# A front end's steps issued one per half step from its beginning (batches 3 to 7) in a fused attention, Fourier and feed-forward kernel

## The chip, the cores and the metric

The kernel runs on one core of a Trainium2 chip. The metric is the device time of one execution in microseconds (us), as the median of several runs. The engines are PE (TensorE), DVE (VectorE), ACT (ScalarE), POOL (GpSimd) and SP (SyncE, which here issues nearly all DMAs). Each engine works through its own list of instructions in the order of the list.

## The reference

For each of 8 batches (576 tokens, 8 heads of width 64): keys and values are averaged over groups of 8 tokens, softmax attention is done against the 72 pooled keys, and the heads' outputs are put side by side to x (576 x 512). Then:

```python
X = np.fft.fft(np.fft.fft(x, axis=1), axis=2)
u = x + np.real(X)
un = (u - mean(u)) / sqrt(var(u) + 1e-6)
out = u + relu(un @ w_ch1) @ w_ch2          # 512 -> 2048 -> 512
```

## The kernel before, in words

**Two kinds of work.** The *feed-forward* work (function `ffn`) is a chain of blocks over token columns. A block has 16 slices of the hidden dimension; each slice has a first product (`g`, line 687, 12 matmuls) and a second one (`acc`, line 671, 12 matmuls). One such dozen is a **half step**. Every product is split into high and low parts (unh, unl for the activations, w1h/w1low and w2h/w2low for the weights), so 12 matmuls are 3 combinations by 4 chunks. The low weight parts are read back from DRAM for each slice (`w1low`, `w2low`, line 210).

The *front end* of a batch (generator `fe(b)`) does the attention, the Fourier part and the normalisation. Its steps end at each `yield`. PE's parts of it have names by stage, with the batch's number: psS (scores), psT, psV, psR (transposes), psX (values), psA and psB (channel transform), psQ and psP (sequence transform), psM (mean), psVar (variance). 20 steps lead to `yield "U"`; before it nothing of the batch's half of the ring is written. Behind it come psQ, then psP (at its last one `yield "free"`), then the mean step with `centre`, and the variance with three Newton steps.

**The ring.** U, unh and unl hold two batches side by side (1152 columns). After batch 0, blocks of 384 columns run over the ring: three blocks for batches 1 and 2 (half steps 64 to 159), three for 3 and 4 (160 to 255), three for 5 and 6 (256 to 351), and two blocks of 288 for batch 7 (352 to 415). The middle block of a round needs the columns of both batches: half steps 192 and 288 are the first that need batch 4 and batch 6. Batch 4's half of the ring is free from half step 160 on, batch 6's from 256 on (table `free`, line 709).

**What a front end does behind psP.** When the last psP matmul is done: X takes the transform (L565, L566 on DVE), POOL makes the sums and differences in U (L582, L583), DVE adds the two even parts (`s`, L575), ACT and DVE split that sum (L577, L578), PE forms the mean in two column halves (psM, L598 and L599), DVE subtracts it half by half (X, L600), ACT rounds the four tiles to unh (L590), and unl is the rest (L591: tiles 0 and 1 on DVE, tiles 2 and 3 on POOL). The first products of the block then use unh and unl.

**The order.** The driver loop (line 769 on) runs through the half steps; after each, `advance(pos)` lets every running front end go on until its count of steps reaches `upto`. A front end begins when the one before it yields "free". Behind "U" it goes one step per half step from `free[b]` on, in both versions. The framework's scheduler then orders each engine's list: it places a front end's instruction where it reckons it ready, so the lists do not stand exactly as the program was written.

Of the kernel before, what the change touches and what calls it, by code (L numbers as in the profile page):

```python
# [80 lines left out]
def tile_kernel(ctx: ExitStack, tc: tile.TileContext, qt, kt, vm, vr, w1, w2, cad, cbd, mkd, out):  # L81
# [627 lines left out]
    free = {1: 0, 2: 64, 3: 128, 4: 160, 5: 224, 6: 256, 7: 320}  # L709
    npre = 20  # L710
# [31 lines left out]
    def start(b, pos):  # L742
        if b < B:
            run[b] = [fe(b), 0, pos, None]

    def advance(pos):
        for b in sorted(run):
            r = run[b]
            if r[3] is None:
                upto = (pos + 1 - r[2]) * npre / max(free[b] - 1 - r[2], 24)  # L750
            else:
                upto = r[3] + pos - max(free[b], r[2]) + 1 if pos >= free[b] else 0
            while r[1] < upto:
                said = next(r[0], "end")
                r[1] += 1
                if said == "U":
                    r[3] = r[1]
                    r[2] = pos
                    break
                if said == "free":  # L760
                    start(b + 1, pos)
                if said == "end":
                    del run[b]
                    break
# [4 lines left out]
    pos = 0  # L769
    for blk in blocks():  # L770
        for _ in ffn(*blk):
            for _ in range(2):
                if done_w < need(pos):
                    prep_w(done_w)
                    done_w += 1
            advance(pos)
            pos += 1
# [109 lines left out]
```

## Time and profile before

| | |
|---|---|
| median of 3 runs | 1124.24 us (1123.67 to 1126.21) |
| the profiled execution's own time | 1127.34 us |
| its span, first to last instruction | 1125.6 us |
| granted TensorE clock, mean | 0.965 |
| PE busy | 1051.0 us (93%), 6484 matmuls |
| DVE, ACT, POOL busy | 629.9, 421.2, 253.1 us |

Times of instructions are counted from the span's start. A row of a timeline gives start, duration, engine, line, operation, output<-inputs and how many followed each other; in square brackets stands how long the engine was idle before, and what ended it. Matmuls are pipelined: the time that one takes from the next is the distance of their starts, not the duration in the row. A row of windows gives the busy time of each engine in a stretch, the granted clock, the DMA share and GB/s.

### The profile page before, as it was taken

How to read it: one execution, taken by the hardware profiler on the slowest of the kernel's cores; microseconds unless marked ns; L12 is line 12 of the kernel's file. 1: busy time of each engine (PE TensorE's matmuls, PEld its weight loads, DVE VectorE, ACT ScalarE, POOL GpSimd, SP SyncE). 2: the span in 40 equal slices, each digit the busy share in tenths (PEclk: the TensorE clock that was granted, in tenths of full speed). 3: DMA queues.
4: the chain of work that ended last, by engine and by line, in shares of the span. 5: the costliest groups of instructions: out<-in, count | busy, mean ns of one | idle time of the engine just before them, and what ended most of it. 6: DMA issues, size and time to landing. Idle time of an engine off the chain costs nothing.

```text
span 1125.6 us, 17476 instructions
## 1 busy us (share of the span) xinstructions
PE 1051.0 (93%) x6484; PEld 1010.6 (90%) x6484; DVE 629.9 (56%) x1228; ACT 421.2 (37%) x1140; POOL 253.1 (22%) x256
## 2 busy tenths in 40 slices
PE   6657898999999999999979999999997999999997
PEld 5446877999999999999968999999986999999997
DVE  7686886856366463664548456565467544353122
ACT  6577864443233332333314333144333342131110
POOL 4473355301140022300232003220024000120000
PEclk8568999999999999999989999999998999999999
DMA  6748987655434454445533446345452434345563
GB/s 221 255 155 258 302 296 232 193 182 163 128 117 149 145 157 132 122 143 153 150 102 106 122 126 195 102 117 160 135 173 58 117 101 133 91 124 180 167 189 97
DMA packets 91877, 175.79 MB, mean 156 GB/s; under 512 B 10128, under 2 KB 17296, under 8 KB 91536
## 3 DMA queue, kind: packets, MB, share of 16 engines
q1 hardware_dynamic: 91504, 172.01, 49.4%
q0 software_dynamic: 288, 2.66, 0.6%
q8 instruction: 51, 0.84, 0.3%
q14 instruction: 34, 0.28, 0.1%
HBM read 156.81 MB, written 17.83 MB: 155 GB/s over the span
## 4 chain that ended last, share of the span: by engine, by line
PE 78%; DVE 6%; DMA 5%; POOL 4%; ACT 3%; issue 3%; SPq 0%; DVEq 0%; POOLq 0%; ACTq 0%
PE acc L671 32%; PE g L687 32%; PE psS L327 3%; PE psX L408 3%; DMA k<-in_kt 2%; PE psA L517 2%; DMA wst<-in_w 1%; PE psP L550 1%; PE psB L533 1%; PE psT L365 1%; POOL U L582 1%; DVE wd L195 1%; POOL k L262 1%; POOL U L583 1%; PE psQ L550 1%
## 5 line engine op out<-in xcount | busy, mean ns | idle before, releaser
L692 DVE SCALAR_TENSOR_TENSOR hl<-g,hh 128x384 fp32r<-128x384 f32 (+1 forms) x208 | 108.5, 522 | 205.2 <-ACT hh L691 201.1
L691 ACT ACTIVATE hh<-g 128x384 fp32r<-128x384 f32 (+1 forms) x208 | 96.6, 465 | 299.5 <-PE g L687 286.7
L671 PE MATMUL acc<-hh,w2h 128*128 128x384 f32 (+1 forms) x832 | 191.4, 330 | 3.5 <-DVE U L702 2.8
L671 PE MATMUL acc<-hh,w2low 128*128 128x384 f32 (+1 forms) x832 | 188.5, 327 | 0.0
L671 PE MATMUL acc<-hl,w2h 128*128 128x384 f32 (+1 forms) x832 | 180.9, 327 | 2.0 <-DVE hl L692 1.9
L687 PE MATMUL g<-unh,w1low 128*128 128x384 f32 (+1 forms) x832 | 176.7, 329 | 4.7 <-DMA w1low<-w1l 4.7
L687 PE MATMUL g<-unl,w1h 128*128 128x384 f32 (+1 forms) x832 | 176.4, 328 | 2.7 <-DVE unl L591 2.1
L687 PE MATMUL g<-unh,w1h 128*128 128x384 f32 (+1 forms) x832 | 174.6, 328 | 0.0
L671 PEld LDWEIGHTS acc<-hh,w2h 128*128 128x128 f32 x832 | 142.7, 189 | 6.9 <-ACT hh L691 3.0
L687 PEld LDWEIGHTS g<-unh,w1low 128*128 128x128 f32 x832 | 140.7, 190 | 6.6 <-DMA w1low<-w1l 5.5
L687 PEld LDWEIGHTS g<-unl,w1h 128*128 128x128 f32 x832 | 140.5, 189 | 6.0 <-DVE unl L591 3.4
L671 PEld LDWEIGHTS acc<-hh,w2low 128*128 128x128 f32 x832 | 143.8, 189 | 0.2
L671 PEld LDWEIGHTS acc<-hl,w2h 128*128 128x128 f32 x832 | 140.3, 189 | 3.3 <-DVE hl L692 3.1
L687 PEld LDWEIGHTS g<-unh,w1h 128*128 128x128 f32 x832 | 140.4, 190 | 0.4
L344 POOL TENSOR_TENSOR t<-t,sm 128x720 f32<-128x720 f32 x32 | 44.8, 1401 | 258.3 <-DVE sm L343 227.7
L262 POOL TENSOR_TENSOR k<-k 128x288 f32<-128x288 f32 (+1 forms) x56 | 38.7, 690 | 94.4 <-DMA k<-in_kt 69.3
L327 PE MATMUL psS<-kpb,q 128*128 128x144 f32 x280 | 45.9, 305 | 6.6 <-DVE X L600 6.4
L582 POOL TENSOR_TENSOR U<-X,U 128x576 f32<-128x576 f32 (+1 forms) x16 | 23.5, 1480 | 118.9 <-DVE X L566 118.9
L327 PEld LDWEIGHTS psS<-kpb,q 128*128 128x128 f32 x280 | 42.6, 206 | 8.0 <-DVE X L600 7.0
L329 DVE TENSOR_REDUCE mx<-psS 128x6 f32<-128x432 f32 x64 | 33.3, 527 | 15.7 <-PE psS L327 15.3
L341 DVE TENSOR_REDUCE sm<-t 128x10 f32<-128x720 f32 x28 | 25.2, 899 | 16.9 <-ACT t L340 16.5
L517 PE MATMUL psA<-ca,f 128*128 128x258 f32 (+1 forms) x144 | 25.3, 307 | 8.9 <-ACT f L477 8.9
(205 smaller groups left out, 1442.5 us busy)
## 6 DMA issues: line engine op xcount, KB each, us to landing
w1low<-w1l SPq DMA_DIRECT2D x208, 256.0 KB, 2.7
w2low<-w2l SPq DMA_DIRECT2D x208, 256.0 KB, 2.9
wst<-in_w SPq DMA_DIRECT2D x30, 512.0 KB, 5.1
q<-in_qt SPq DMA_DIRECT2D x28, 288.0 KB, 3.1
k<-in_kt SPq DMA_DIRECT2D x28, 288.0 KB, 2.9
v<-in_vm SPq DMA_DIRECT2D x28, 256.0 KB, 2.9
out<-U SPq DMA_DIRECT2D x18, 384.0 KB, 3.7
w1l<-wd SPq DMA_DIRECT2D x16, 256.0 KB, 4.7
```

What stands on the lines that cost most here:

```text
L262: nc.gpsimd.tensor_tensor(out=out if n == 1 else src[:, :, 0:n], in0=src[:, :, 0] if n == 1 else src[:, :, 0:n], in1=src[:, :, 1] if n == ...
L327: nc.tensor.matmul(ps[:, c * W2J:(c + 1) * W2J], lhsT=q[:, r0:r0 + P], rhs=kpb[g % 2], start=True, stop=True)
L329: nc.vector.tensor_reduce(out=mx[:, c0:c0 + n], in_=pv, op=ALU.max, axis=AX.X, negate=b in SM)
L341: nc.vector.tensor_reduce(out=sm, in_=t, op=ALU.add, axis=AX.X)
L344: ins = nc.gpsimd.tensor_tensor(out=t, in0=t, in1=sm.unsqueeze(3).broadcast_to([P, 5, 2, J]), op=ALU.mult)
L408: nc.tensor.matmul(ps, lhsT=w, rhs=a, start=(i == 0), stop=(i == len(mm) - 1))
L517: nc.tensor.matmul(ps, lhsT=w, rhs=a, start=(n == 0), stop=(n == len(mm) - 1))
L582: engine(1 - j, UE).tensor_tensor(out=a, in0=e, in1=o, op=ALU.add)
L671: nc.tensor.matmul(acc[e], lhsT=w[:, e], rhs=h, start=(f == f0 and x == 0), stop=(f == f1 - 1 and x == 2))
L687: nc.tensor.matmul(ps, lhsT=w[:, c], rhs=x[:, ti, cl], start=(n == 0), stop=(n == 11))
L691: nc.scalar.activation(hh, ps, AF.Relu)
L692: nc.vector.scalar_tensor_tensor(out=hl, in0=ps, scalar=0.0, in1=raw(hh), op0=ALU.max, op1=ALU.subtract)
```

## The change

Only the number of steps that `advance` allows before "U" is changed:

```diff
             if r[3] is None:
-                upto = (pos + 1 - r[2]) * npre / max(free[b] - 1 - r[2], 24)
+
+                upto = (pos + 1 - r[2]) * (npre / (free[b] - 1) if b == 2 else 1)
             else:
                 upto = r[3] + pos - max(free[b], r[2]) + 1 if pos >= free[b] else 0
```

`r[2]` is the half step at which the front end began, `npre` is 20. Batch 2 began before the loop (`r[2]` is 0), and its number stays what it was. By the program, batch 3 begins at half step 67 and reached "U" at 127, and now at 86; batch 4 begins at 131 and reached it at 159, now at 150; batch 5 begins at 163: 223, now 182; batch 6 begins at 227: 255, now 246; batch 7 begins at 259: 319, now 278. No instruction is added or removed.

In PE's list, counted in half steps (feed-forward matmuls that stand ahead, divided by 12), the stages stand here:

| batch | first psS | first psT | last psB | psP_2 | last psM |
|---|---|---|---|---|---|
| 3 before, now | 92.4, 87.0 | 102.1, 99.8 | 135.9, 131.3 | 141.1, 136.5 | 144.8, 140.2 |
| 4 before, now | 141.1, 136.5 | 156.3, 148.7 | 189.9, 181.8 | 192.0, 186.9 | 192.0, 190.6 |
| 5 before, now | 192.0, 186.9 | 201.1, 199.2 | 235.9, 230.2 | 241.1, 235.3 | 244.8, 239.0 |
| 6 before, now | 241.1, 235.3 | 256.3, 247.7 | 288.0, 279.4 | 288.0, 284.6 | 288.0, 288.0 |
| 7 before, now | 288.0, 284.6 | 297.2, 295.0 | 330.7, 325.2 | 335.8, 330.4 | 339.2, 333.6 |

PE's list at the block that first needs batch 4 (g1_2112_0 and g1_2112_1 are its first two first products, acc1728 is the block ahead, psS5 batch 5's scores), before:

```order
L550 MATMUL psP4_2_5718<-cb_71,A0_5462 128x290 x3
L550 MATMUL psP4_2_5718<-cb_71,A1_5463 128x290 x3
L550 MATMUL psP4_2_5718<-cb_71,AB2_5464 128x290
L598 MATMUL psM4_5779<-s_5750,avg_74 128x288
L598 MATMUL psM4_5783<-s_5750,avg_74 128x288
L599 MATMUL psM4_5779<-s_5751,avg_74 128x288
L599 MATMUL psM4_5783<-s_5751,avg_74 128x288
L327 MATMUL psS5_3_0_5832<-kpb1_76,q5_3_5761 128x144 x3
L327 MATMUL psS5_3_3_5838<-kpb1_76,q5_3_5761 128x144 x2
L687 MATMUL g1_2112_0_6501<-unh_83,w1h_68 128x384
L687 MATMUL g1_2112_1_6548<-unh_83,w1h_68 128x384
```

and now, from the same stage on:

```order
L550 MATMUL psP4_2_5718<-cb_71,A0_5351 128x290 x3
L550 MATMUL psP4_2_5718<-cb_71,A1_5352 128x290 x3
L550 MATMUL psP4_2_5718<-cb_71,AB2_5353 128x290
L327 MATMUL psS5_3_0_5776<-kpb1_76,q5_3_5761 128x144 x3
L671 MATMUL acc1728_0_3_5623<-hl_6547,w2h6_2090 128x384
L687 MATMUL g1_1728_14_6599<-unh_83,w1h7_2013 128x384 x4
L687 MATMUL g1_1728_14_6599<-unl_84,w1h7_2013 128x384 x4
L687 MATMUL g1_1728_14_6599<-unh_83,w1low_6562 128x384 x4
L671 MATMUL acc1728_0_0_5620<-hh_6579,w2h6_2090 128x384
L671 MATMUL acc1728_0_1_5621<-hh_6579,w2h6_2090 128x384
```

Before, no feed-forward matmul stood between psP4_2 and the block's first products; now 61 do, with the four psM4 and psS5's ten among them. At the block of batch 6 (g1_3264) it stood before as at batch 4's, with all of psQ6 and the last two tiles of psB6 also behind the old block's last matmul; now psP6_2 stands like this:

```order
L671 MATMUL acc2880_0_2_8290<-hh_9247,w2low_9199 128x384
L550 MATMUL psP6_2_8386<-cb_71,A0_8019 128x290 x3
L550 MATMUL psP6_2_8386<-cb_71,A1_8020 128x290 x3
L550 MATMUL psP6_2_8386<-cb_71,AB2_8021 128x290
L327 MATMUL psS7_3_0_8444<-kpb1_76,q7_3_8429 128x144 x3
L671 MATMUL acc2880_0_3_8291<-hh_9247,w2low_9199 128x384
L671 MATMUL acc2880_0_0_8288<-hl_9248,w2h6_2090 128x384
L671 MATMUL acc2880_0_1_8289<-hl_9248,w2h6_2090 128x384
```

and 41 feed-forward matmuls, four psM6 and ten psS7 stand between it and g1_3264's first.

DVE's list at the same place. Before, from the end of batch 6's mean on (L600 subtracts it, L591 is unl, L329 and L338 belong to batch 7's scores):

```order
L578 TENSOR_TENSOR s_8419<-s_8417,s_8418 128x576
L600 TENSOR_TENSOR X_80<-U_81,psM6_8447 128x4x288
L600 TENSOR_TENSOR X_80<-U_81,psM6_8451 128x4x288
L329 TENSOR_REDUCE mx_8498<-psS7_3_0_8500 128x6
L591 TENSOR_TENSOR unl_84<-X_80,unh_83 128x576
L338 TENSOR_TENSOR t7_3_8497<-psS7_3_0_8500,mx_8498 128x432
L591 TENSOR_TENSOR unl_84<-X_80,unh_83 128x576
```

Now the first L600 is followed by a sum of batch 7 (L341) and the four L701 of the block that ends, and from the last of these on it reads:

```order
L701 TENSOR_TENSOR acc2880_0_3_8291<-acc2880_0_3_8291,rb_82 128x384
L600 TENSOR_TENSOR X_80<-U_81,psM6_8478 128x4x288
L342 TENSOR_SCALAR sm_8443<-sm_8443 128x10
L702 TENSOR_TENSOR U_81<-U_81,acc2880_0_0_8288 128x384
L329 TENSOR_REDUCE mx_8550<-psS7_2_0_8552 128x6
L702 TENSOR_TENSOR U_81<-U_81,acc2880_0_1_8289 128x384
L702 TENSOR_TENSOR U_81<-U_81,acc2880_0_2_8290 128x384
L702 TENSOR_TENSOR U_81<-U_81,acc2880_0_3_8291 128x384
L343 RECIPROCAL sm_8443<-sm_8443 128x10
L591 TENSOR_TENSOR unl_84<-X_80,unh_83 128x576
L338 TENSOR_TENSOR t7_2_8549<-psS7_2_0_8552,mx_8550 128x432
L591 TENSOR_TENSOR unl_84<-X_80,unh_83 128x576
```

So the eight instructions that end the old block (L701, L702) stood ahead of batch 6's psQ work before, and now stand among its last instructions.

## The prediction

> **What bounds the kernel now.** I read the page's first two parts, then a table of windows, then PE's waits.
>
> ```profile
> span 1125.6 us, 17476 instructions
> PE 1051.0 (93%) x6484; PEld 1010.6 (90%) x6484; DVE 629.9 (56%) x1228; ACT 421.2 (37%) x1140; POOL 253.1 (22%) x256
> PEclk8568999999999999999989999999998999999999
> ```
>
> The clock falls twice after the start, in slices 21 and 31. Windows around these places:
>
> ```profile
> 250.00:566.00 316.00, 316.00 (x1914) 311.08 (x1914) 173.27 (x346) 108.73 (x296) 61.93 (x62) 1.00 0.47 142
> 606.00:833.00 227.00, 227.00 (x1375) 223.69 (x1374) 124.46 (x247) 79.20 (x220) 38.03 (x40) 1.00 0.46 140
> 572.00:606.00 34.00, 24.98 (x136) 22.35 (x134) 24.17 (x39) 9.66 (x18) 12.66 (x8) 0.85 0.25 79
> 838.00:868.00 30.00, 20.91 (x114) 17.69 (x113) 23.91 (x38) 9.04 (x17) 12.66 (x8) 0.89 0.23 72
> ```
>
> Columns: stretch, its length, busy PE, PEld, DVE, ACT, POOL, then granted clock, DMA share, GB/s. From 250 us on PE is busy without a gap (316.00 of 316.00), except in two stretches, where it idles 9.0 and 9.1 us and the clock drops. These are half steps 192 and 288, the first that need batch 4 and batch 6. PE's waits from 250 us to the end name what came late there, and nothing else; the three longest (us in total, times, longest):
>
> ```profile
> PE psS L327 <- DVE X L600: 6.4, 2, 3.2
> PE psM L598 <- ACT s L577: 5.9, 2, 3.2
> PE psP L550 <- DVE U L566: 1.5, 1, 1.5
> ```
>
> So the even batches reach the boundary with the whole of psP, mean and centring still to do, and PE follows that chain bare. What each boundary costs is read from PE's timeline, first at batch 4:
>
> ```profile
> 579.02 0.96 PE L550 MATMUL psP<-cb,A 128*2 128x290 f32 x6
> 579.81 0.30 PE L550 MATMUL psP<-cb,AB 98*2 98x290 f32 x1
> ...
> 583.40 0.29 PE L550 MATMUL psP<-cb,AB 98*128 98x290 f32 x1
> 586.93 0.85 PE L598 MATMUL psM<-s,avg 128*128 128x288 f32 x2 [3.24 <-ACT s L577]
> ...
> 592.05 2.77 PE L327 MATMUL psS<-kpb,q 128*128 128x144 f32 x10 [3.16 <-DVE X L600]
> ...
> 600.45 0.86 PE L671 MATMUL acc<-hh,w2h 128*128 128x384 f32 x4
> 601.14 0.88 PE L671 MATMUL acc<-hh,w2low 128*128 128x384 f32 x4
> ```
>
> From 579.02 to 600.45 are 21.4 us. Work in it: 21 psP at 0.133 (0.79 for 6), 4 psM at the same, 10 psS at 0.105 (a row below), 24 first products at 0.174 (0.69 for 4): 2.8 + 0.5 + 1.05 + 4.2 = 8.55. **Lost at batch 4: 12.9 us**, half-rate matmuls included. At batch 6:
>
> ```profile
> 838.37 1.56 PE L533 MATMUL psB<-ca,f 128*128 128x256 f32 x12
> ...
> 863.42 0.87 PE L671 MATMUL acc<-hh,w2h 128*128 128x384 f32 x4
> ```
>
> 25.05 us, less the same 8.55, 12 psB at 0.12 and 14 psQ at 0.133 (3.3): **lost at batch 6: 13.2 us**. Together 26.1 us, which is all that PE loses after 250 us.
>
> **The change part by part.** Instructions, bytes and the path's work stay. What moves is the place of the front ends in every list; worth something only at the two boundaries, since elsewhere PE has no gap to win.
>
> *Cover now.* Batch 4's psP_2 now has 61 feed-forward matmuls, 4 psM and 10 psS programs (20 matmuls in the trace, which runs each of these twice) between itself and the block: 61 x 0.174 + 0.5 + 20 x 0.105 = 13.2 us. Batch 6's has 41: 9.75 us. What this must hide is the chain from psP_2 to the last unl. The trace shows it in a batch that was in time, batch 3, with PE full:
>
> ```profile
> 450.89 0.30 PE L550 MATMUL psP<-cb,AB 98*128 98x290 f32 x1
> 451.03 0.90 PE L327 MATMUL psS<-kpb,q 128*128 128x144 f32 x6
> 451.67 0.79 PE L687 MATMUL g<-unh,w1h 128*128 128x384 f32 x3
> ...
> 460.37 0.29 PE L599 MATMUL psM<-s,avg 128*128 128x288 f32 x1
> ```
>
> (0.64 us for six psS is the 0.105.) On the other engines:
>
> ```profile
> 456.96 0.46 DVE L338 TENSOR_TENSOR t<-psS,mx 128x288 f32<-128x288 f32 x1
> 458.29 0.90 DVE L341 TENSOR_REDUCE sm<-t 128x10 f32<-128x720 f32 x1 [0.87 <-ACT t L340]
> 459.11 1.34 DVE L600 TENSOR_TENSOR X<-U,psM 128x1152 f32<-128x1152 f32 x1
> 460.37 0.17 DVE L342 TENSOR_SCALAR sm<-sm 128x10 f32<-128x10 f32 x1
> 461.04 1.30 DVE L600 TENSOR_TENSOR X<-U,psM 128x1152 f32<-128x1152 f32 x1
> 462.36 2.40 ACT L590 CAST unh<-X 128x576 fp32r<-128x576 f32 x4 [2.95 <-DVE X L600]
> 463.07 1.43 DVE L591 TENSOR_TENSOR unl<-X,unh 128x576 fp32r<-128x576 f32 x2 [0.74 <-ACT unh L590]
> 464.27 2.92 POOL L591 TENSOR_TENSOR unl<-X,unh 128x576 fp32r<-128x576 f32 x2 [1.58 <-ACT unh L590]
> ```
>
> psP ends at 451.19; the first unh is there 11.8 us later, DVE's two unl after 13.3, POOL's second after 16.0. This is the length to hide.
>
> *Batch 4.* Its neighbours on DVE and POOL are now those of batch 3, and psM stands equally far behind psP_2 (3.7 half steps). The block's list takes the last unl of its first product as its 15th matmul, 14 x 0.174 behind the first: 13.2 + 2.4 = 15.6 us against 16.0. One L329 (0.61) between DVE's two unl moves that one to 13.9, needed at 15.0. **Left: 0.4 us**, of 12.9.
>
> *Batch 6.* Only 9.75 us of cover, and DVE now has the old block's end among the last steps:
>
> ```profile
> 838.05 1.96 DVE L701 TENSOR_TENSOR acc<-acc,rb 128x384 f32<-128x384 f32 x4 [0.73 <-PE acc L671]
> 839.91 1.01 DVE L702 TENSOR_TENSOR U<-U,acc 128x384 f32<-128x384 f32 x2
> ...
> 856.89 0.61 DVE L329 TENSOR_REDUCE mx<-psS 128x6 f32<-128x432 f32 x1 [0.63 <-PE psS L327]
> ...
> 858.60 1.64 DVE L591 TENSOR_TENSOR unl<-X,unh 128x576 fp32r<-128x576 f32 x1
> ```
>
> Counted from psP_2's end: the first psM half stands behind 28 feed-forward matmuls, done at 6.5; L600 6.7 to 8.05; L341 to 8.95; four L701 (1.96) to 10.9; second L600 to 12.2; the four unh to 14.6 (2.40); meanwhile on DVE L342, four L702 (2.0), L329, L343 to 15.0; first unl, beside POOL's, 1.64, to 16.6; L338 to 17.2; second unl 0.75 to 17.9. PE takes that one as its 11th matmul, at 9.75 + 1.74 = 11.5. **Left: 6.4 us** of 13.2. From both sides: with the template's 13.3 alone 1.8 (then POOL's 16.0 decides: 3.8), and no less than nothing; if every wait were kept, 13.2. I take 6.4, since each row is in the list that is now there. What is queued behind this wait in PE's list are both first products of the block (24 matmuls) and then its second ones; what was late before, psM, is no longer: the end of the old block on DVE is what is late next.
>
> *Clock.* The gap before batch 6's block is some 3 us (unh at 12.8, cover 9.75), then a second of about 2. The trace had such gaps:
>
> ```profile
> 584.00:589.00 5.00, 1.70 (x4) 1.00 (x4) 3.17 (x6) 0.67 (x1) 4.89 (x3) 0.59 0.38 141
> 589.00:594.00 5.00, 1.95 (x8) 1.95 (x9) 2.72 (x3) 0.70 (x2) 1.61 (x2) 0.50 0.00 0
> ```
>
> There the clock was at half after gaps of 1.46, 3.24 and 3.16 us with little between. Now the gap follows a full stretch. At half rate the 24 first products cost at most 24 x 0.174 = 4.2 more, else nothing; I take 1.0. The Trainium skill (TensorE: Matmul & The Clock Gate, "Why this matters for your kernels") tells to keep gaps between matmul bursts under about 3 us, since one idle window halves the clock; by it the drop comes, and the sum would end 3 us higher, at 1110. The trace agrees for three gaps together; no row shows one alone.
>
> *Denser steps.* Batch b+1's scores now fall between batch b's psM and psVar. That adds some 3.4 us of DVE work (L329, L338, L341, L342) in front of hl, which gates PE's next second product. What hides it: DVE is 56% busy on the page, and where it was fullest PE lost nothing:
>
> ```profile
> 325.00:350.00 25.00, 25.00 (x153) 24.96 (x152) 21.90 (x41) 12.64 (x25) 6.08 (x5) 1.00 0.53 163
> ```
>
> Without that cover it is 3.4 for each of five batches. Bounds 0 and 17; I take 0.5, by this row. The loads of q, k and v go through SP's queue, ahead of low weights:
>
> ```profile
> SPq L210 <- PE g L687: 337.2, 146, 4.8
> SPq L243 <- PE psS L327: 31.8, 11, 15.2
> ```
>
> Low weights wait for a buffer anyway (337.2 us in 146 waits, 2.3 each), and PE had no gap from it after 250 us; the 15.2 was in a boundary stall. Nothing for it. At the end, batch 7's front end is finished some 70 half steps before the last block; moving it by 5 gains nothing.
>
> *Sum.* Gone 26.1; left 0.4 + 6.4 + 1.0 + 0.5 = 8.3; gain 17.8. The profiled execution took 1127.34 us (span 1125.6 and 1.7 around it): 1109.5 for such a one. The median of the runs is 3.1 lower: 1124.24 - 17.8 = **1106.4 us**.
>
> **The rivals.**
>
> *Both boundaries all but close.* If DVE's old block end slips between the waits of ACT, batch 6 is left with POOL's 3.8 or less: gone 26.1, left 0 to 4.2, so 1098 to 1102; 1100. For it: DVE was never the cause of a gap outside the boundaries. Against: the lists have nothing else to do there. Chance 0.17.
>
> *New waits in the denser part.* PE's list is in order, and one psT or psX that isn't ready holds all behind it. Two or three us (the gaps above were 1.5 to 3.2) in each of batches 3 to 7 give back 10 to 15 of the gain: 1116 to 1121. Against: the 316.00 of 316.00, which holds batch 4's scores to psB, whose 20 steps were already given only 28 half steps. Chance 0.12.
>
> *It does not do what it says.* A front end cannot pass the one ahead (X, psVar), so the chain could be as late as ever and the wait only stand at psT or psB instead of psM: 1122 to 1126. Against: in PE's list psP4_2 moves up by 5.1 half steps and psP6_2 by 3.4, past feed-forward work. Chance 0.04.
>
> *Slower.* SP's queue: q waits for the psS that reads its buffer, and w1low and w2low stand behind it. Mean wait 31.8 / 11 = 2.9 us; if each of the 20 loads of q in batches 3 to 7 held the queue 1.5 us beyond the low weights' lead, PE would lose 30 us against the gain of 17.8: 1136. It decides from 0.9 us a load on (20 x 0.9 = 17.8). Against: the loads' places among the low weights move by a few slices only. Chance 0.03.
>
> **How the numbers follow.** Forecast 0.64 with 1106.4 and own range 1102 to 1112 (batch 6 left with 3.8 to 9, the clock 0 to 4.2). The other chances are above. The range of 8 in 10 takes most of the first rival and the lower edge of the second: 1099.5 to 1115. A measurement here tells about 0.2% (2.2 us) from no change; faster by more: 0.64 + 0.17 + 0.12 = 0.93; within: 0.04; slower: 0.03.
>
> **What would show it.** Right: no gap at batch 4's block and clock 1.00 there; at batch 6's block PE's waits name unh L590 and unl L591 with 5 to 8 us in all, and psM <- s L577 is gone; PE full elsewhere from 250 us on. Wrong: gaps before psT, psX or hl in batches 3 to 7, w1low as a releaser, or batch 6's wait under 3 or over 10 us.

## The result and the profile after

| | before | now |
|---|---|---|
| median of 4 runs each | 1124.47 us (1123.67 to 1126.21) | 1107.16 us (1105.64 to 1107.96) |
| profiled execution, its span | 1127.34, 1125.6 us | 1107.08, 1105.3 us |
| granted clock, mean | 0.965 | 0.974 |

The ratio is 0.9842, interval 0.9825 to 0.9859: 17.3 us less. Predicted were 1106.4 us and a gain of 17.8. Three lines of the page after, the sums and PE's clock:

```profile
span 1105.3 us, 17483 instructions
PE 1044.3 (94%) x6484; PEld 1005.3 (91%) x6484; DVE 625.3 (57%) x1228; ACT 419.6 (38%) x1140; POOL 254.5 (23%) x256
PEclk8588999999999999999999999999999999999999
```

The counts of these five are those of before; the 7 instructions more are not among them.

Of the two dips of the clock behind the start, no slice shows one now. Windows of the kernel after, columns as before (the two boundaries are the second and the fourth row; with the shorter span the second one lies some 18 us earlier):

```profile
250.00:566.00 316.00, 316.00 (x1923) 310.68 (x1922) 177.56 (x355) 108.80 (x298) 62.54 (x65) 1.00 0.46 139
566.00:606.00 40.00, 38.75 (x231) 37.44 (x230) 30.59 (x52) 15.60 (x32) 12.03 (x9) 1.00 0.45 138
606.00:820.00 214.00, 214.00 (x1305) 210.39 (x1304) 119.61 (x238) 74.52 (x211) 39.57 (x41) 1.00 0.47 139
820.00:850.00 30.00, 25.44 (x137) 23.60 (x137) 24.25 (x38) 11.40 (x23) 14.04 (x10) 0.94 0.38 117
```

Batch 4's boundary is all but closed, at full clock; batch 6's still has 4.6 us without a matmul. PE's waits of the kernel after, from 250 us to the end, this time all of them (us in total, times, longest):

```profile
PE psS L327 <- DVE X L600: 2.4, 1, 2.4
PE g L687 <- DVE unl L591: 2.2, 2, 1.3
PE acc L671 <- DVE U L702: 0.6, 1, 0.6
PE g L687 <- POOL unl L591: 0.4, 1, 0.4
PE acc L671 <- DVE hl L692: 0.2, 1, 0.2
```

The wait of psM for ACT's s (5.9 before) is gone, and the longest of before (6.4) is down to 2.4.

**One yardstick for all runs.** Waits alone leave out matmuls at half clock. So for each profile the distance from each matmul's start to the next is taken, less the median distance of its kind, and summed over the boundary (about 45 to 55 us around it). This "lost" time is 13.0 us at batch 4 and 14.0 at batch 6 before (the prediction, by another count, had 12.9 and 13.2), and 2.4 and 8.1 after: 16.5 us gained. The stretches between the boundaries hold 1.6 to 2.9 us in both. The first 250 us, whose instructions are the same, differ by 4.2 us between these two executions (78.1 and 73.9 lost). Their sum is about the 20.3 by which the two spans differ; the medians, 17.3 apart, are over four runs each.

*Batch 4.* Rows of PE's timeline after, the three with a wait noted there:

```profile
583.95 0.44 PE L687 MATMUL g<-unl,w1h 128*128 128x384 f32 x1 [0.43 <-POOL unl L591]
587.27 0.44 PE L671 MATMUL acc<-hh,w2h 128*128 128x384 f32 x1 [0.60 <-DVE U L702]
588.57 0.96 PE L671 MATMUL acc<-hl,w2h 128*128 128x384 f32 x4 [0.21 <-DVE hl L692]
```

And DVE's of the same kernel:

```profile
581.14 1.95 DVE L701 TENSOR_TENSOR acc<-acc,rb 128x384 f32<-128x384 f32 x4
...
583.88 1.01 DVE L702 TENSOR_TENSOR U<-U,acc 128x384 f32<-128x384 f32 x2
584.80 1.95 DVE L611 TENSOR_TENSOR X<-X 128x576 f32<-128x576 f32 x1
586.67 1.01 DVE L702 TENSOR_TENSOR U<-U,acc 128x384 f32<-128x384 f32 x2
```

The first wait is the forecast one: POOL's second unl is 0.4 us late. The second was not in the prediction. Two of the old block's four L702 now stand behind L611, a step of batch 4's variance (1.95 us; alone it takes 0.74, and POOL's L612 runs beside it from 584.70 to 586.14). Until L702 has read acc, the new block cannot write there. The third wait, for DVE's hl, follows from the same crowded list.

*Batch 6.* PE's timeline after:

```profile
831.42 0.90 PE L327 MATMUL psS<-kpb,q 128*128 128x144 f32 x6
834.68 0.76 PE L327 MATMUL psS<-kpb,q 128*128 128x144 f32 x4 [2.36 <-DVE X L600]
835.38 2.34 PE L687 MATMUL g<-unh,w1h 128*128 128x384 f32 x8
838.65 0.62 PE L687 MATMUL g<-unl,w1h 128*128 128x384 f32 x2 [0.93 <-DVE unl L591]
840.53 1.97 PE L687 MATMUL g<-unl,w1h 128*128 128x384 f32 x5 [1.27 <-DVE unl L591]
```

DVE's:

```profile
829.33 1.35 DVE L600 TENSOR_TENSOR X<-U,psM 128x1152 f32<-128x1152 f32 x1 [0.44 <-PE psM L599]
830.61 0.89 DVE L341 TENSOR_REDUCE sm<-t 128x10 f32<-128x720 f32 x1
831.42 1.95 DVE L701 TENSOR_TENSOR acc<-acc,rb 128x384 f32<-128x384 f32 x4
833.28 1.34 DVE L600 TENSOR_TENSOR X<-U,psM 128x1152 f32<-128x1152 f32 x1
...
835.59 1.48 DVE L702 TENSOR_TENSOR U<-U,acc 128x384 f32<-128x384 f32 x3
...
837.11 1.48 DVE L591 TENSOR_TENSOR unl<-X,unh 128x576 fp32r<-128x576 f32 x1
838.51 0.59 DVE L338 TENSOR_TENSOR t<-psS,mx 128x432 f32<-128x432 f32 x1
839.03 1.45 DVE L591 TENSOR_TENSOR unl<-X,unh 128x576 fp32r<-128x576 f32 x1
```

psP_2 ended at 822.68; DVE's second unl ended at 840.48, 17.8 us later, and 17.9 were predicted. psM's second half was ready at 831.58, yet its L600 began at 833.28, behind four L701. ACT's unh follow it, one every 0.57 us:

```profile
834.65 2.40 ACT L590 CAST unh<-X 128x576 fp32r<-128x576 f32 x4 [4.92 <-DVE X L600]
```

And a window of the kernel after, around the last gap:

```profile
840.50:844.00 3.50, 3.46 (x11) 3.47 (x12) 2.72 (x4) 2.28 (x5) 3.39 (x3) 0.51 0.00 0
```

Where do the 8.1 us go? The matmul that takes DVE's second unl began at 840.53, 17.85 us after psP_2; without a wait it would have stood at 11.5 by the prediction's count. These 6.4 us are the three waits (2.36 + 0.93 + 1.27 = 4.6) and 1.8 us of matmuls at full clock that could not follow closely, half of it at the eight first products, two for each unh, which began 0.29 us apart instead of 0.174. The last 1.7 us were lost behind the last wait, in the stretch at half clock, which began at 840.55 and lasted 3.4 us.

### The profile page after: what moved, and what is told of

Read it like the earlier page. It is cut to its first block, busy times and chain, and to the rows that moved or that the text cites. A ratio compares the mean times of both kernels' runs of the same rounds, so it can differ in the third digit from the quotient of the medians.

```text
span 1105.3 us, 17483 instructions
## 1 busy us (share of the span) xinstructions
PE 1044.3 (94%) x6484; PEld 1005.3 (91%) x6484; DVE 625.3 (57%) x1228; ACT 419.6 (38%) x1140; POOL 254.5 (23%) x256
## 4 chain that ended last, share of the span: by engine, by line
PE 82%; DVE 7%; DMA 4%; ACT 3%; POOL 1%; issue 1%; SPq 0%; DVEq 0%; POOLq 0%; ACTq 0%
PE acc L671 34%; PE g L687 33%; PE psX L408 3%; PE psA L517 2%; PE psS L327 2%; PE psP L550 2%; PE psB L533 1%; PE psT L365 1%; PE psQ L550 1%; DMA wst<-in_w 1%; DVE unl L591 1%; DVE wd L195 1%; DMA w1low<-w1l 1%; DVE wd L194 1%; DMA w2low<-w2l 1%
## 5 line engine op out<-in xcount | busy, mean ns | idle before, releaser
L671 PEld LDWEIGHTS acc<-hl,w2h 128*128 128x128 f32 x832 | 140.2, 188 | 3.2 <-DVE hl L692 2.9
L582 POOL TENSOR_TENSOR U<-X,U 128x576 f32<-128x576 f32 (+1 forms) x16 | 20.9, 1308 | 128.4 <-DVE X L566 128.4
L329 DVE TENSOR_REDUCE mx<-psS 128x6 f32<-128x432 f32 x64 | 33.1, 525 | 11.7 <-PE psS L327 11.4
L340 ACT ACTIVATE t<-t 128x720 f32<-128x720 f32 x28 | 22.5, 803 | 37.1 <-DVE t L338 36.8
L341 DVE TENSOR_REDUCE sm<-t 128x10 f32<-128x720 f32 x28 | 25.2, 899 | 16.7 <-ACT t L340 16.5
## 6 DMA issues: line engine op xcount, KB each, us to landing
q<-in_qt SPq DMA_DIRECT2D x28, 288.0 KB, 3.0
k<-in_kt SPq DMA_DIRECT2D x28, 288.0 KB, 2.9
```

Source lines behind the costliest of these rows:

```text
L329: nc.vector.tensor_reduce(out=mx[:, c0:c0 + n], in_=pv, op=ALU.max, axis=AX.X, negate=b in SM)
L340: nc.scalar.activation(t, t, AF.Exp, scale=1.0 / 64.0)
L341: nc.vector.tensor_reduce(out=sm, in_=t, op=ALU.add, axis=AX.X)
L671: nc.tensor.matmul(acc[e], lhsT=w[:, e], rhs=h, start=(f == f0 and x == 0), stop=(f == f1 - 1 and x == 2))
```

## Experiments

Two accounts were set against each other. *Cover*: feed-forward matmuls now stand between a batch's psP_2 and the block that needs it, and hide the chain from psP to unl; what is left at batch 6 is DVE's crowded list. The rivals are named run by run. Each time is compared with runs of the kernel before on the same chip; their medians were 1125.2 (the first four runs below), 1125.18 (the fifth and sixth) and 1124.38 (the last four). The formula of the kernel before is meant where a diff says `old`.

**The even batches alone.**

```diff
-                upto = (pos + 1 - r[2]) * (npre / (free[b] - 1) if b == 2 else 1)
+                upto = pos + 1 - r[2] if b in (4, 6) else old
```

> One step per half step for batches 4 and 6 alone; 3, 5 and 7 keep the old pace. Theory (cover): a boundary costs the chain from psP_2 to unl less the feed-forward work that PE's list holds behind psP_2, and the odd batch's pace counts because the even one begins at its psP. In this list psP4_2 stands at half step 189.8 (26 feed-forward matmuls of cover, 4.5 us) and psP6_2 still at 288.0. Left: about 7.5 us at batch 4 and 11 at batch 6, so some 1117 us. Rival (own pace): only the even batches were late, so their own pace is what counts, and the time is that of the full change, 1107. Second rival (no help unless all move): 1124.

Measured: 1117.51 us (1116.32 to 1118.83), ratio 0.9936 (0.9917 to 0.9955). Lost: 6.4 at batch 4, 12.5 at batch 6. In PE's list psP4_2 stands at half step 189.8 with 27 feed-forward matmuls behind it, psP6_2 at 288.0 with none. Cover's number was met, with parts that missed both ways (7.5 and 11 expected). A front end's own pace is not all of it: batch 6's psP_2 stayed where it was although its own pace was changed. That it cannot pass the batch ahead would explain this; no run shows it by itself.

**The odd batches alone** (3, 5, 7 in the same line).

> One step per half step for batches 3, 5 and 7 alone; 4 and 6 keep the old pace. Theory (cover): batch 4 begins 4.6 half steps sooner (136.5), psP4_2 stands at 189.0 (36 feed-forward matmuls, 6.3 us), psP6_2 at 288.0 as before. Left: 5 to 6.5 us at batch 4 and 11 at batch 6, so some 1116 us. Rival (own pace): the odd batches were never late, so nothing is gained, 1124.

Measured: 1119.8 us (1118.93 to 1120.97), ratio 0.9956 (0.9941 to 0.9971). Lost: 9.3 and 12.7. Neither number was met (1116 and 1124). At batch 4, 36 feed-forward matmuls stand behind psP4_2, nine more than in the run above, and still more is lost. PE's timeline of this run:

```profile
581.82 1.00 PE L327 MATMUL psS<-kpb,q 128*128 128x144 f32 x6 [1.24 <-DVE X L600]
585.01 1.31 PE L327 MATMUL psS<-kpb,q 128*128 128x144 f32 x4 [2.19 <-DVE X L600]
...
590.86 1.14 PE L687 MATMUL g<-unl,w1h 128*128 128x384 f32 x5 [1.27 <-DVE unl L591]
```

These are the waits that the change has at batch 6. Batch 5's scores come close, the old block's four L701 stand between the two L600 of DVE, and its second L600 ends 12.5 us after psP_2 (9.2 with the even batches alone), its second unl 18.3 (13.6). So the theory with a fixed length of chain failed: more cover did not help where the chain was longer, and what else stands in DVE's list lengthens it. This is read from the lists; a run below tests it at batch 6. The two halves of the change give 7.7 and 5.4 us, less than its 17.3 together: batch 6's boundary opens only with both.

**Half-size pieces on top of the change.** Batches 0 and 1 do the sums, unh and unl in two column halves (set `HZ`), so that unh can begin after the first L600.

```diff
-HZ = {0, 1}
+HZ = {0, 1, 4, 6}
```

> The change, and batches 4 and 6 do the sum for the mean and the centring in two column halves, as batches 0 and 1 do. The first block that needs an even batch uses 192 of its columns, all in the first half. Theory (chain): unl of the first half is there some 12 to 13 us behind psP_2 and not 16 to 18, against 13.2 us of cover at batch 4 and now about 11 at batch 6 (psP6_2 at 283.9), the 15th matmul coming 2.4 later: the boundaries lose 0 to 1 and 0 to 2 us, where the change alone lost 2.4 and 7.9; 1098 to 1101 us. Rival (whole tiles): the block waits for both halves, and eight smaller instructions take the place of four, so nothing is gained or a little lost, 1107 to 1109.

Measured: 1103.84 us (1102.6 to 1107.51), ratio 0.9821 (0.9793 to 0.985). Lost: 2.5 and 2.9. Every wait for X, unh or unl is gone, but the time is 3 to 6 us above what was expected, for a wait that stood second now comes first. PE's waits of this run, all of them from 250 us on:

```profile
PE acc L671 <- DVE U L702: 2.6, 4, 1.2
PE acc L671 <- DVE hl L692: 0.4, 1, 0.4
```

DVE has the four L702 behind its last unl, and PE needs their accumulators. (The expectations of this run and of two later ones counted the lost time a little lower: 7.9, 2.3 and 2.7 for what is 8.1, 2.5 and 2.9 here.)

**The same pieces without the change.**

> The kernel before (old pace), with the sum and the centring of batches 4 and 6 in halves. PE's list still has no feed-forward matmul behind psP_2 at both boundaries. Theory (chain less cover): the bare chain of 14.8 us gets some 5 to 6.5 us shorter at each boundary, since the first half's sums on POOL and the first half's unl are done sooner: 1111 to 1115 us. Rival (only the place in the list counts): 1124.

Measured: 1124.82 us (1123.31 to 1127.67), ratio 0.9998 (0.9984 to 1.0012). My account failed here, the rival held. Lost: 12.5 and 12.6, against 13.0 and 14.0. PE's longest waits in this run:

```profile
PE psM L598 <- ACT s L577: 5.9, 4, 2.8
PE psS L327 <- DVE X L600: 4.4, 2, 2.2
PE acc L671 <- ACT hh L691: 2.0, 2, 1.1
```

The waits for unh and unl became one for hh, and a score of batch 5 stands ahead of the block's first products and waits for the second L600. Whether that score was the cause, the next run tells.

**The same, and batches 5 and 7 begin later**, so that no score stands there.

```diff
-                if said == "free":
+                if said == ("z" if b in (4, 6) else "free"):
```

> The kernel before, with the half-size chain for batches 4 and 6, and with batches 5 and 7 beginning at the last step of 4 and 6 instead of at "free". Theory that the first score matmul of the next batch, which stands ahead of the block's first products in PE's list and waits for the second L600, ate what the half-size chain should have given: it now stands behind them, so that wait (4.4 us in all) is gone and the time falls by 2 to 5 us, to 1119 to 1122. Rival, that with PE standing still the chain from psP to unl has no slack at all and the hold on psS only covers a wait for unh and unl which comes anyway: no change, 1123 to 1126, with the wait now named unh L590 or unl L591. Either way far from 1107: the feed-forward work is not there to cover the chain.

Measured: 1128.62 us (1127.08 to 1131.89), ratio 1.0036 (1.0022 to 1.005). The score is not the cause: the rival's wait, for unh, has come, though its number was missed too. PE's three longest waits of this run:

```profile
PE psM L598 <- ACT s L577: 6.0, 4, 2.8
PE g L687 <- ACT unh L590: 5.3, 2, 2.6
PE psB L533 <- DVE f L478: 1.6, 1, 1.6
```

The wait for psS is gone and one for unh has come in its place. Behind it stands POOL, in DVE's timeline of this run:

```profile
586.55 2.62 DVE L600 TENSOR_TENSOR X<-U,psM 128x1152 f32<-128x1152 f32 x2 [1.43 <-POOL U L583]
```

POOL's eight half-size sums (L582, L583) end 7.3 us after psP_2, four whole ones 6.9 before: the first half's are no sooner (the first L600 begins 6.6 us after psP_2, 7.0 before), and the halves shorten only what comes behind L600. At batch 4 the first products do begin 8.5 us after psP_2 here and 10.8 before, since the ten psS, which took 2.4 us at half clock, no longer stand ahead of them. But now they run at half clock themselves. Windows of the run here:

```profile
582.50:592.50 10.00, 6.40 (x18) 5.22 (x19) 8.54 (x9) 4.11 (x11) 8.15 (x10) 0.52 0.03 11
```

PE's timeline of the kernel before, the block's first products:

```profile
594.45 1.79 PE L687 MATMUL g<-unh,w1h 128*128 128x384 f32 x7
```

and its window:

```profile
585.50:594.50 9.00, 4.14 (x15) 3.45 (x15) 4.92 (x6) 1.87 (x4) 5.11 (x4) 0.50 0.11 42
```

Half clock lasted some 10 us in both; before, it was nearly over as the first products began; here 4 us of them fell into it, and the lost time at batch 4 is 13.0 in both. The 3.4 us that the median is above the kernel before come from batch 6 (17.6 lost, 14.0 before), whose front end began later, with waits in psB.

**Half-size pieces and unl on POOL, without the change** (the second edit stands below, at unl).

> The kernel before, with the same two edits that brought the change to 1099 (half-size chain for batches 4 and 6, their unl on POOL), and without the change. Theory that these edits are worth something only where feed-forward work covers most of the chain: 1123 to 1126 (POOL's unl come later than DVE's, the stall is as long). Rival, that they are worth as much by themselves (the 8 us that they gave on top of the change): 1115 to 1117.

Measured: 1123.6 us (1120.91 to 1126.95), ratio 0.9986 (0.9967 to 1.0005): no difference that can be told. Lost: 12.6 and 13.5.

**The change again**, on the chip of the next three runs.

> The change itself once more, as the yardstick on the chip of the next three: 1106 to 1108 us, or 0.984 of the kernel before.

Measured: 1108.75 us (1107.48 to 1109.96), ratio 0.9855 (0.9835 to 0.9874). Lost: 2.4 and 6.5; so batch 6's boundary by itself differs by 1.6 between two executions of one kernel. The chain is the same: the second unl's matmul begins 17.85 us after psP_2 in both. What differs is the clock: its 3.4 us at half began 12.8 us after psP_2 here and was over before the last wait; in the first execution it began 17.9 us after psP_2, behind that wait.

**Batch 7 begins later**, at batch 6's mean instead of its psP, on top of the change: its scores leave the place between batch 6's steps.

```diff
-                if said == "free":
+                if said == ("z" if b == 6 else "free"):
```

> The change, but batch 7's front end begins at batch 6's mean and not at its last psP: its scores leave DVE's list ahead of batch 6's block, and both L600 then stand ahead of the old block's L701. PE's cover stays at 41 feed-forward matmuls and loses five psS (1.05 us). Theory (what is left at batch 6 comes from the work that stands between its steps in DVE's list): the second DVE unl is there some 14.7 us behind psP_2 and not 17.8, wanted at 10.5: 4 to 5 us lost where the change lost 7.9; 1103.5 to 1105.5 us. Rival (the cover alone sets it): 1 us less cover, so 1107 to 1108.

Measured: 1104.73 us (1103.4 to 1107.7), ratio 0.9823 (0.9799 to 0.9847), 4.0 us below the change. Lost: 2.4 and 5.3, so 1.2 to 2.8 us of the 4.0 are seen at batch 6 (6.5 and 8.1 with the change); the rest is within the spread of the runs. DVE's timeline of this run:

```profile
827.59 2.62 DVE L600 TENSOR_TENSOR X<-U,psM 128x1152 f32<-128x1152 f32 x2 [1.43 <-PE psM L599]
830.12 1.95 DVE L701 TENSOR_TENSOR acc<-acc,rb 128x384 f32<-128x384 f32 x4
```

Both L600 now run ahead of the four L701, the first unl begins at 832.96 instead of 837.11 (10.9 and 14.4 us after psP_2), and PE's wait for X is gone. What stays is 0.92 and 1.27 for unl. So the order of DVE's list is a part of what was left, as the prediction had it, and the length of the cover not all.

**unl of batches 4 and 6 on POOL**, on top of the change.

```diff
-                engine(ti, UL).tensor_tensor(out=ul, ...)
+                (nc.gpsimd if b in (4, 6) else engine(ti, UL)).tensor_tensor(out=ul, ...)
```

> The change, with all four unl of batches 4 and 6 on POOL, none on DVE. In DVE's list both L600 of batch 6 then stand ahead of L701, and PE's list has 50 feed-forward matmuls behind psP6_2, 11.3 us of cover. Theory: the chain now ends with four POOL instructions of 1.45 us, 17.6 us behind psP_2, wanted at 13.8: about 4 us left at batch 6; at batch 4 about 2 as with the change; 1102.5 to 1105 us. Rival (POOL's four in a row are a longer tail than two by two): 1107 or more.

Measured: 1108.46 us (1105.24 to 1111.43), ratio 0.9852 (0.9824 to 0.9879), the same as the change. Lost: 2.0 and 7.1. The waits for X, for L702 and for hl are gone from PE, and one line is left (PE's waits of this run):

```profile
PE g L687 <- POOL unl L591: 3.9, 5, 1.3
```

Four whole unl on one engine come one after another; POOL's timeline of this run at batch 6:

```profile
834.62 6.03 POOL L591 TENSOR_TENSOR unl<-X,unh 128x576 fp32r<-128x576 f32 x4
```

My expectation failed, and the rival's time came, but not by its reason alone. POOL's last unl ended 18.2 us after psP_2, where the theory had 17.6 and wanted 13.8: 4.4 us, about the 4 that it expected to be left. Some 2.6 of the 7.1 were lost behind that, at half clock, which the theory had left out. The clock's windows show for how long:

```profile
839.00:843.00 4.00, 2.75 (x9) 2.42 (x10) 1.93 (x5) 2.33 (x6) 3.49 (x4) 0.55 0.21 78
843.00:846.00 3.00, 3.00 (x11) 3.00 (x11) 2.73 (x3) 1.34 (x4) 1.22 (x1) 0.50 0.49 131
```

**Both: half-size pieces and unl on POOL**, on top of the change.

> The change, batches 4 and 6 in column halves as before, and their unl all on POOL. With halves alone the boundaries lost 2.3 and 2.7 us, all of it PE's next acc waiting for the old block's L702, which stood behind unl in DVE's list. Theory (DVE's list): without unl on DVE, L702 is done some 1.5 to 2 us sooner and the first half's unl (four of 0.75 us on POOL) still in time: 0 to 1.5 us left in all, 1098 to 1101 us. Rival (POOL late): the first half's unl come last, 1103 to 1106.

Measured: **1099.15 us** (1098.38 to 1100.13), ratio 0.9767 (0.9747 to 0.9788), 9.6 us below the change on the same chip, and 25.2 below the kernel before. Lost: 0.2 and 0.7. Windows of this run at the boundaries:

```profile
566.00:606.00 40.00, 40.00 (x244) 39.92 (x243) 30.17 (x54) 16.56 (x37) 17.47 (x20) 1.00 0.46 140
...
820.00:850.00 30.00, 30.00 (x181) 29.54 (x180) 22.51 (x41) 12.44 (x29) 18.03 (x20) 1.00 0.50 152
```

No wait of PE is left from 250 us to the end. Alone on top of the change, POOL gave nothing and the halves 4 to 6 us (21.4 below the kernel before, the change 17.3 and 15.6); the halves move the chain ahead and leave DVE's L702 late, POOL takes from DVE what stood ahead of L702. Without the change the same two edits gave nothing that can be told. A lever is worth something only as far as what stands next to it in time is out of the way.

## Why the prediction was right, point by point

- *What bounds the kernel.* Right. All that was gained from 250 us on lies at the two boundaries (16.5 of 27.0 us in the profiles); elsewhere PE was and stayed full.
- *Cover at batch 4: 0.4 left.* The POOL wait was 0.43, as worked out, though both of its ends moved: POOL's second unl ended 16.5 us after psP_2 and not 16.0, and the matmul that takes it could have begun at 15.8 and not 15.6. But 2.4 were lost. The step that failed is "left: 0.4": it followed the new block's needs through unl alone and not through its accumulators, so the old block's L702, which DVE now does late, was missed there (0.60), and hl after it (0.21); the rest of the 2.4 is the slow start of matmuls around these three gaps, at full clock.
- *Cover at batch 6: 6.4 left.* The term held: 6.4 us were lost up to the matmul that takes DVE's second unl. The chain came out to 0.1 us (17.8 and 17.9), and the instructions that delay it were the ones named; that it is so close is partly luck. DVE came to its first unl 0.6 us sooner than reckoned (14.4 and 15.0 us after psP_2), and the second took 1.45 us and not 0.75, since POOL's second ran beside it. The waits have other names than forecast: psS of batch 7 is ahead of the first products in PE's list and waits for the second L600 (2.36). That place cost next to nothing by itself, for the first unh was there only 0.7 us later, and the first product began with it.
- *Clock: 1.0.* The drop came, for one stretch of 3.4 us, and cost 1.7, within the bound of 4.2. The rule of the Trainium skill (TensorE: Matmul & The Clock Gate, "Why this matters for your kernels") foresaw the drop and its sum 1110; the forecast took a quarter of the price and came nearer to the time, 1107.16. Which of the two came nearer hung on when the clock fell: in the change's second execution the same stretch was over before the last wait and cost nothing. One reading of the prediction was loose: in the kernel before the clock did not fall after gaps of 1.46, 3.24 and 3.16 us, but some 1.2 us into the second of them (its window from 584.00 to 589.00 has a mean of 0.59). So that trace does not bear the rule out either.
- *Denser steps: 0.5.* Nothing was lost there: 316.00 of 316.00 and 214.00 of 214.00. The loads on SP's queue cost nothing either; no wait of PE names one. One figure there is misread: the 70 half steps behind batch 7's front end reach to the end of all blocks; the block that first needs it begins at 352, 13 behind its last psM. Moving it gained nothing all the same.
- *Sum.* 10.5 left instead of 8.3, of 27.0 instead of 26.1 at stake: 16.5 in the profiles, 17.3 by the medians, 17.8 forecast. Batch 4 cost 2.0 more than forecast and the clock 0.7 more, the denser steps 0.5 less, and there was 0.9 more to gain. That the medians come as near as 0.5 is luck on top, within the spread of the runs.
- *What would show it.* psM's wait is gone and PE is full elsewhere, as named. At batch 4 the clock stayed at 1.00, but there were gaps (0.43, 0.60, 0.21). At batch 6 the waits are 4.6 us, for X and unl; 5 to 8 for unh and unl were named, and under 3 as the sign of being wrong.
- *The rivals.* "Both boundaries all but close" named POOL's unl as the floor; the run with the halves and POOL reached its time (1099.15) by another way. "New waits in the denser part" did not come. "Does not do what it says" fell for the change as a whole; its reason, that a front end cannot pass the one ahead, would fit batch 6 when only the even batches are moved. "Slower" did not come either.

What stays open: why the first 250 us lose 73 to 78 us from one execution to another of the same instructions, and what sets the moment at which the clock falls, which decided over 1.7 us at batch 6.

## What to carry to other kernels

When PE stands still at a point where it needs a result, first see how much independent work can stand between the producer and that point; shortening the chain itself gave nothing here while PE waited bare for an earlier link, and 9.6 us once the work covered it. After such a change list what else the next block needs (accumulators, buffers that a score holds), in every engine's list: the second-latest becomes the wait. A step that an engine does for the old block beside the new block's chain is counted with the chain.

## What the runs showed of the hardware that was not expected

- The clock fell at gaps that are each short. In the kernel after: 2.36, 0.93 and 1.27 us within 8.2 us, then 3.4 us at half. In the second execution of the same kernel it fell 0.8 us after the 2.36 alone. With unl on POOL it fell when two gaps of 0.75 us lay behind it, two matmuls between them, and a third of 1.25 was beginning, and stayed at half for 6.8 us. With the half-size pieces gaps of 1.16, 0.21 and 0.36 us left it at 1.00, as a window of that run shows:

```profile
835.00:845.00 10.00, 8.27 (x45) 7.06 (x44) 10.00 (x21) 5.56 (x14) 4.89 (x5) 1.00 0.59 187
```

  So the longest gap alone doesn't decide; where the limit is, these runs don't tell. The rule of the Trainium skill (TensorE: Matmul & The Clock Gate, "Why this matters for your kernels"), to avoid gaps of more than about 3 us, is too generous for these: no gap here was longer than 2.36 us.
- A stall that ends earlier can leave the same time lost: the half-clock period, 10.2 us at batch 4 both with half-size pieces and later scores and in the kernel before, then covers the first products instead of the wait.
- Two unl of 128x576 that run at the same time lengthen one or the other: at batch 4 DVE's kept its 0.75 us and POOL's beside it took 2.04 (the next one, alone, 1.43), at batch 6 DVE's took 1.48 and 1.45. In the kernels before and after, wherever two of this size overlapped, DVE's ended 0.61 or 0.62 us after POOL's, or POOL's 1.27 to 1.30 after DVE's. That looks as if one had waited for the other and then run nearly its whole length; no run here tests it.
